# A float64 weight conversion issued as a pipeline over slots, with four load buffers and in-place results, and the attention product moved to the end of a unit

## The chip, the cores and the metric

The kernel runs on one core of a Trainium2 chip. The metric is the time of one execution on the device in microseconds (us). The engines have names of their own: TensorE (PE; its weight loads are listed as PEld), VectorE (DVE), ScalarE (ACT), GpSimd (POOL), and the queue of SyncE (SP), which here only issues DMAs. ScalarE issues some DMAs too (ACTq).

## The reference, cut to what matters

```python
# q, k, v: (8, 8, 576, 64) float32
scores = (q @ k.T) / 8;  keep = scores >= rowmax(scores) - tau          # the rest: -1e9
attn = softmax over the kept;  x = (attn @ v) as (8, 576, 512)
# w_tok1 (576, 256), w_tok2 (256, 576), w_ch1 (512, 1536), w_ch2 (1536, 512): float64
h = relu(x.T @ w_tok1) @ w_tok2;  u = x + h.T
out = u + relu(u @ w_ch1) @ w_ch2
```

The four weight arrays arrive as float64, and the kernel turns them into float32 itself, from their two 32-bit words.

## The kernel before, in words

The program is written out by hand in one order, and every engine executes its own instructions in that order. The main loop (L513) runs over **units**. A unit is a batch, a pair of head pairs, and a tile of 128 query rows; there are 18 units to a batch and 144 in all. Iteration u does, in this order:

- `scores(u)` (L272): the score matmuls (L286) into two PSUM tiles, a maximum for each (L291, VectorE), and from it a bias (L292, GpSimd). The next unit's scores need the same PSUM, so they wait for this unit's L301.
- `norm(u-1)` (L307): two small VectorE steps (L310, L311), and two multiplications on GpSimd (L314).
- The transposed weights of attention for unit u-2. In batch 0 this is `turn`: TensorE transposes (L337) and copies out of PSUM (L339, two or three on VectorE). In later batches it is `turn_blocks`: one VectorE transpose (L348), and, when a group of units is complete, 16 DMAs from the SP queue (L358). GpSimd's `split_middle` (L367) belongs here.
- `fill(0.4)`: from batch 1 on, steps of the mixer of an earlier batch are taken from a queue (`todo`) until a share of the unit's quota is used up. The steps are the transposes of x (`turn_x`, L412, copies on ScalarE L413), `tok1` (L422, L423), `tok2` (L429, its sum on VectorE L433), `ch1` (L451, L452) and `ch2` (L463, L467, L472, store L473). They are priced at 0.44, 4.3, 0.97, 1.7 and 2.6 to 3.0 us.
- `weight(4)`, or `weight(1)` in batch 0: steps of the conversion.
- `weigh(u)` (L295): the two L301 activations and the two exponentials L304 on ScalarE.
- `fill(0.3)`, then the due `values` (L370): the product with v (L388, L393) of a group completed one unit before (batch 0) or two units before, and its copy by ScalarE (L398). After the last one of a batch, `push` puts that batch's mixer steps into `todo` and sets the quota to an even share for 17 units. Then `fill(0.3)`.
- `weight(3)`, or `weight(1)` in batch 0, and then the loads of q, k and v (L106, L114) and the transposes of `prep` (L268).

**The conversion.** There are 31 pieces of at most 128x512 values, each converted in three steps. Each step issues one VectorE instruction, L161, L164 or L167. The first step also issues two ScalarE instructions ahead of it: L159, which scales the low words in the load buffer, and L160, which squares the high words for a test of tiny values. The third step adds the rounding on GpSimd (L168), which writes the weight tile, and then issues the load of the piece three further on (L196, SP queue). That load waits for L168, since it goes into the same buffer. There are three load buffers, two buffers for the result in work, and one for the squares, all in `scratch`. The VectorE steps of a piece wait for its load and for L160; L160 waits for the preceding piece's L167, which reads the one buffer of squares. `need` lets a mixer step force the conversion of its piece.

Of the kernel before, what the change touches and what calls it, by code (L numbers as in the profile page):

```python
# [9 lines left out]
F32 = mybir.dt.float32  # L10
U32 = mybir.dt.uint32
I32 = mybir.dt.int32
I64 = mybir.dt.int64
AF = mybir.ActivationFunctionType
ALU = mybir.AluOpType
# [6 lines left out]
def kernel(  # L22
# [105 lines left out]


# [4 lines left out]
    NRAW = 3  # L134
    raw_at = [scratch[:, 2 * WMAX * i : 2 * WMAX * (i + 1)] for i in range(NRAW)]
    a_at = [scratch[:, 2 * WMAX * NRAW + WMAX * i : 2 * WMAX * NRAW + WMAX * (i + 1)] for i in range(2)]
    sq_at = scratch[:, 2 * WMAX * NRAW + 2 * WMAX : 2 * WMAX * NRAW + 3 * WMAX].bitcast(F32)
    turn_of = [0]

    def like(x, dst):  # L140
        if len(dst.shape) == 2:
            return x
        return x.rearrange("p (a b) -> p a b", a=dst.shape[1])

    def f64_to_f32(dst, raw, rows, n):

        lo, hi = raw[:, :, 0], raw[:, :, 1]
        a = a_at[turn_of[0] % 2][0:rows, 0:n]
        h2 = sq_at[0:rows, 0:n]
        turn_of[0] += 1
        af = a.bitcast(F32)
        nc.scalar.activation(out=lo.bitcast(I32), in_=lo, func=AF.Copy, scale=2.0**-29)  # L159
        nc.scalar.activation(out=h2, in_=hi.bitcast(F32), func=AF.Square)  # L160
        yield nc.vector.tensor_scalar(  # L161
            out=a, in0=hi, scalar1=3, scalar2=0x3FFFFFFF, op0=ALU.logical_shift_left, op1=ALU.bitwise_and
        )
        yield nc.vector.scalar_tensor_tensor(  # L164
            out=a, in0=hi, scalar=0xC0000000, in1=a, op0=ALU.bitwise_and, op1=ALU.bitwise_or
        )
        nc.vector.scalar_tensor_tensor(out=af, in0=h2, scalar=2.0**-30, in1=af, op0=ALU.is_ge, op1=ALU.mult)  # L167
        nc.gpsimd.tensor_tensor(  # L168
            out=dst.bitcast(I32), in0=like(a.bitcast(I32), dst), in1=like(lo.bitcast(I32), dst), op=ALU.add
        )  # L170
# [13 lines left out]

    raws = {}

    def load_piece(i):
        dst, src = pieces[i]
        rows = dst.shape[0]
        n = 1  # L190
        for d in dst.shape[1:]:
            n *= d
        wide = src.dtype == I64
        raw = raw_at[i % NRAW][0:rows, 0 : n * (2 if wide else 1)]
        raw = raw.bitcast(src.dtype)
        nc.sync.dma_start(out=like(raw, dst), in_=src)  # L196
        raws[i] = raw, rows, n

    def weight_ops():
        for i, (dst, src) in enumerate(pieces):  # L200
            raw, rows, n = raws.pop(i)
            if src.dtype == I64:
                for _ in f64_to_f32(dst, raw.bitcast(U32).rearrange("p (n w) -> p n w", w=2), rows, n):
                    yield
            else:
                yield
                yield
                nc.gpsimd.tensor_copy(out=dst, in_=like(raw, dst))
            if i + NRAW < len(pieces):
                load_piece(i + NRAW)  # L210
            yield

    wops = weight_ops()
    steps_done = 0

    def weight(n):

        nonlocal steps_done
        for _ in range(n):
            if next(wops, wops) is wops:  # L220
                return
            steps_done += 1

    def need(i):

        weight(3 * i + 3 - steps_done)
# [6 lines left out]
    load_v(1)  # L233

# [166 lines left out]
    def token_mlp(b):  # L401
# [4 lines left out]
        def turn_x(t):  # L406
            M = MT[t]
            if t == 0:
                s["x"] = work.tile([P, NT, DM], F32, tag="x", bufs=1, name=f"x_{b}")
            ps = ps_tr.tile([P, MAIN], F32, tag="tr", name=f"tx_{b}_{t}").rearrange("p (c x) -> p c x", c=NP)  # L410
            for p in range(NP):
                nc.tensor.transpose(out=ps[0:M, p, :], in_=xT[:, p, o + t * P : o + t * P + M], identity=ident)  # L412
            nc.scalar.copy(out=s["x"][0:M, t, :], in_=ps[0:M].rearrange("q p d -> q (p d)"))  # L413

        def tok1(m):
            need(2)
            if m == 0:
                s["a"] = work.tile([P, NTK, DM], F32, tag="a", bufs=1, name=f"a_{b}")
            ps = ps_mm.tile([P, DM], F32, tag="mm", name=f"t1_{b}_{m}")
            for t in range(NT):  # L420
                M = MT[t]
                nc.tensor.matmul(ps, lhsT=w1[0:M, t, P * m : P * m + P], rhs=s["x"][0:M, t, :], start=(t == 0), stop=(t == NT - 1))  # L422
            nc.scalar.activation(out=s["a"][:, m, :], in_=ps, func=AF.Relu)  # L423
# [89 lines left out]
    for u in range(len(units) + LAG + 4):  # L513
# [11 lines left out]
        if 0 < u <= len(units):  # L525
            norm(u - 1)
        if back:
# [16 lines left out]
        weight(4 if b_now else 1)  # L544
        if on:
            weigh(u)
        if b_now:
            fill(0.3)
        while due and due[0][0] <= u:
            _, b, p, c = due.popleft()  # L550
            values(b, p, c)
            if p == NP - 1 and c == 1:
                push(b)
        if b_now:
            fill(0.3)
        weight(3 if b_now else 1)
# [10 lines left out]
    weight(10000)  # L567
# [30 lines left out]
```

## Time and profile before

| | |
|---|---|
| time, median of 11 runs | 1419.58 us (1418.18 to 1427.12) |
| the profiled execution | 1419.88 us, of which the span is 1417.8 us |
| TensorE busy | 1342.8 us, 95% of the span |
| VectorE, ScalarE, GpSimd busy | 583.7, 588.2 and 345.1 us |
| mean granted TensorE clock | 0.982 |
| L161, L164, L167, mean at 128x512 | 457, 1115 and 712 ns |
| L159, L160, mean at 128x512 | 676 and 665 ns |
| L168, mean at 128x512 | 1350 ns |
| L358: 896 DMAs of 72 KB and 224 of 36 KB | 2.0 and 1.9 us from issue to landing |
| load of a 512 KB weight piece (L196) | 3.7 us from issue to landing |

The page gives each engine's busy time, which says little by itself: most of it lies beside other engines' work. The row of the span in 40 slices (35.4 us each) tells where TensorE isn't busy. The view of waits says who waited for whom, the timeline shows single instructions, and the table by windows gives the busy time of each engine in a stretch. The starts of the score matmuls in the timeline date the units: unit 18, the first of batch 1, starts at 98.56 us, units 19 to 27 at 107.61, 116.08, 130.85, 142.17, 156.95, 171.36, 180.97, 193.79 and 204.88 us.

### The profile page before, as it was taken

The page shows a single profiled execution, that of the slowest core. Times are in us where ns is not written, and L with a number is a line of the kernel's source. Part 1 is how long each engine was busy: PE and PEld are TensorE (multiplying, and loading weights), DVE is VectorE, ACT ScalarE, POOL GpSimd, SP SyncE. Part 2 cuts the span into 40 slices and gives each one's busy share as a digit, 9 for nine tenths or more (in the row PEclk, how much of TensorE's full clock was granted, in tenths as well). Part 3 has the DMA queues.
Part 4 walks back from the last instruction along what each step waited for, and adds up shares of the span by engine and source line. Part 5 has one row for each costly group of instructions (what it writes and reads, how often), then busy time and mean ns, then how long its engine had stood idle before and what let it go on. Part 6 is the DMA issues. An engine that isn't in the chain of part 4 may idle for free.

```text
span 1417.8 us, 19495 instructions
## 1 busy us (share of the span) xinstructions
PE 1342.8 (95%) x6866; PEld 831.0 (59%) x6866; DVE 583.7 (41%) x1009; ACT 588.2 (41%) x1328; POOL 345.1 (24%) x681
## 2 busy tenths in 40 slices
PE   6777699978999999999999999999999999999998
PEld 3444465635656567565656466566656466566675
DVE  5888654344444444434343443434333443201000
ACT  5776453444445444443434454353334344220110
POOL 4565332222222222221221222222122222100000
PEclk8997899999999999999999999999999999999999
DMA  6344544353455434343343434443433433300000
GB/s 135 85 117 127 155 127 104 91 124 80 107 121 115 102 89 105 96 101 85 90 100 81 112 81 114 102 100 72 102 88 79 112 92 78 88 9 15 8 8 23
DMA packets 257376, 128.34 MB, mean 91 GB/s; under 512 B 208064, under 2 KB 221376, under 8 KB 257280
## 3 DMA queue, kind: packets, MB, share of 16 engines
q1 hardware_dynamic: 131632, 111.46, 29.8%
q10 hardware_dynamic: 125648, 15.64, 6.9%
q8 instruction: 55, 0.90, 0.3%
q14 instruction: 41, 0.34, 0.1%
HBM read 43.25 MB, written 9.44 MB: 37 GB/s over the span
## 4 chain that ended last, share of the span: by engine, by line
PE 80%; DVE 7%; SPq 5%; DMA 4%; ACT 3%; issue 1%; POOL 0%; ACTq 0%; DVEq 0%; POOLq 0%
PE c L467 26%; PE c L451 23%; PE sc L286 10%; PE pv L393 7%; SPq L358 5%; PE t L429 3%; PE t L422 3%; PE pv L388 2%; DVE mx L291 2%; DVE T L348 2%; PE tx L412 2%; DMA eT<-T 1%; PE c L463 1%; DMA lk<-in_k_dram 1%; ACT e L301 1%
## 5 line engine op out<-in xcount | busy, mean ns | idle before, releaser
L451 PE MATMUL c<-xT,wc 128*128 128x256 f32 (+1 forms) x1920 | 407.2, 364 | 2.4 <-ACT g L452 1.1
L291 DVE TENSOR_REDUCE mx<-sc 128x1 f32<-128x576 f32 x288 | 204.6, 751 | 486.4 <-PE sc L286 486.3
L467 PE MATMUL c<-wc,g 128*128 128x512 f32 x864 | 389.5, 597 | 0.0
L451 PEld LDWEIGHTS c<-xT,wc 128*128 128x128 f32 x1920 | 332.5, 191 | 76.3 <-issue 29.9
L292 POOL TENSOR_SCALAR bias<-mx,toff 128x1 f32<-128x1 f32 x288 | 76.1, 265 | 804.0 <-DVE mx L291 751.7
L301 ACT ACTIVATE e<-sc,bias 128x576 f32<-128x576 f32 x288 | 198.6, 738 | 169.7 <-POOL bias L292 157.9
L467 PEld LDWEIGHTS c<-wc,g 128*128 128x128 f32 x864 | 157.7, 190 | 177.2 <-issue 175.8
L452 ACT ACTIVATE g<-c 128x256 f32<-128x256 f32 (+1 forms) x240 | 86.8, 362 | 386.9 <-PE c L451 375.7
L304 ACT ACTIVATE e<-e,ntau 128x576 f32<-128x576 f32 x288 | 220.1, 772 | 0.0
L314 POOL TENSOR_SCALAR e<-e,rr 128x576 f32<-128x576 f32 x288 | 213.7, 754 | 17.6 <-DVE rr L311 4.5
L286 PE MATMUL sc<-kT,qT 64*128 64x288 f32 (+1 forms) x1280 | 194.7, 436 | 20.7 <-ACT e L301 11.4
L348 DVE STREAM_TRANSPOSE T<-e 128x1152 f32<-128x1152 f32 x126 | 172.5, 1369 | 16.1 <-DMA eT<-T 12.1
L286 PEld LDWEIGHTS sc<-kT,qT 64*128 64x128 f32 (+1 forms) x1280 | 106.3, 179 | 102.2 <-issue 49.5
L393 PE MATMUL pv<-eT,lv 128*64 128x256 f32 x1024 | 124.3, 386 | 0.0
L472 DVE COPY o<-c 128x512 f32<-128x512 f32 x36 | 24.6, 684 | 192.7 <-PE c L467 192.7
L393 PEld LDWEIGHTS pv<-eT,lv 128*64 128x64 f32 x1024 | 75.8, 140 | 38.6 <-issue 3.2
L429 PE MATMUL t<-w,a 128*128 128x288 f32 x256 | 78.3, 435 | 17.3 <-DVE xT L433 15.4
L422 PE MATMUL t<-x,w 128*128 128x512 f32 (+1 forms) x160 | 75.0, 606 | 0.0
L429 PEld LDWEIGHTS t<-w,a 128*128 128x128 f32 x256 | 46.9, 198 | 42.2 <-DVE xT L433 20.4
L398 ACT COPY xT<-pv 128x256 f32<-128x256 f32 x64 | 23.8, 371 | 108.5 <-PE pv L393 108.4
L433 DVE TENSOR_TENSOR xT<-xT,t 128x288 f32<-128x288 f32 x64 | 27.9, 442 | 95.9 <-PE t L429 95.9
L304 ACT ACTIVATION_READ_ACCUMULATOR e<-e,ntau 128x1 f32 x288 | 56.9, 198 | 0.0
(43 smaller groups left out, 595.9 us busy)
## 6 DMA issues: line engine op xcount, KB each, us to landing
eT<-T SPq DMA_DIRECT2D x896, 72.0 KB, 2.0
scratch<-in_moe_w_ch_dram SPq DMA_DIRECT2D x24, 512.0 KB, 3.7
lv<-in_v_dram SPq DMA_DIRECT2D x32, 288.0 KB, 3.3
out_dram<-o SPq DMA_DIRECT2D x36, 256.0 KB, 2.2
eT<-T SPq DMA_DIRECT2D x224, 36.0 KB, 1.9
lk<-in_k_dram ACTq DMA_DIRECT2D x108, 72.0 KB, 2.7
lq<-in_q_dram ACTq DMA_DIRECT2D x104, 72.0 KB, 2.1
lq<-in_q_dram SPq DMA_DIRECT2D x24, 72.0 KB, 3.3
```

What stands on the lines that cost most here:

```text
L286: nc.tensor.matmul(sc[h][rows, f, 0:HS], lhsT=qT[r, cols], rhs=kT[r, HS * f : HS * f + HS], start=True, stop=True)
L291: nc.vector.tensor_reduce(out=mx[:, c], in_=sc[h][:, :, 0:HS], axis=AX.XY, op=ALU.max)
L301: nc.scalar.activation(out=eh, in_=sc[h][:, :, 0:HS], func=AF.Prelu, bias=bias[:, h : h + 1], scale=SCALE, alpha=STEEP)
L304: nc.scalar.activation(out=eh, in_=eh, func=AF.Exp, bias=ntau, accum_out=rs[:, h : h + 1])
L314: nc.gpsimd.tensor_scalar(out=eh, in0=eh, scalar1=rr[:, h : h + 1], scalar2=1.0, op0=ALU.mult, op1=ALU.mult)
L348: nc.vector.transpose(out=T.rearrange("p (a c n x) -> p c a n x", a=4, c=NK, n=n)[:, :, :, place, :], in_=e.rearrange("p (c a x) -> p c a ...
L393: nc.tensor.matmul(to[r], lhsT=lv[:, j, :], rhs=eT[:, j], start=False, stop=(c == NI - 1), skip_group_check=True)
L422: nc.tensor.matmul(ps, lhsT=w1[0:M, t, P * m : P * m + P], rhs=s["x"][0:M, t, :], start=(t == 0), stop=(t == NT - 1))
L429: nc.tensor.matmul(ps, lhsT=s["a"][:, m, P * c : P * c + P], rhs=w2[:, m, HS * f : HS * f + HS], start=(m == 0), stop=(m == NTK - 1))
L451: nc.tensor.matmul(ps, lhsT=wc1[:, j, c, :], rhs=uT[:, c, GR * i : GR * i + n], start=(c == 0), stop=(c == NCC - 1))
L452: nc.scalar.activation(out=s["g"][:, j, 0:n], in_=ps, func=AF.Relu)
L467: nc.tensor.matmul(flat, lhsT=s["g"][:, j, P * t : P * t + P], rhs=wc2[:, j, :], start=False, stop=(j == NJ - 1), skip_group_check=True)
```

## The change: what it does, and the diff

The conversion becomes a pipeline. A step is a **slot** and issues one VectorE instruction, as before. With it go, in the first slot of piece i, the GpSimd sum of piece i-1 and the load of piece i+3 (there are now four load buffers), and in the second and third slots the two ScalarE instructions of piece i+1. VectorE writes straight into the weight tile, in place. The squares use two buffers, those of the output tile `o`. In batch 0 two slots a unit are issued at the old places. From batch 1 on six are issued, in three pairs: a pair after `norm` and ahead of the transposes, a pair after `fill(0.4)`, and a pair at the end. In this text they are called the first, second and third pair. `values` and `push` stand at the end of the iteration, and one `fill(0.6)` stands for the two of 0.3. `tok1` takes 128 rows for the last tile of tokens too, where it took 64: the other 64 rows of `w1` and of x are zeroed once at the start by GpSimd, and x has a fixed tile.

```diff
+    x_sb = const.tile([P, NT, DM], F32, name="x_sb")
+    nc.gpsimd.memset(x_sb[LAST:P, NI, :], 0.0)
+    nc.gpsimd.memset(w1[LAST:P, NI, :], 0.0)
...
-    NRAW = 3
+    NRAW = 4
...
+        if wide(i):
+            words = raw.bitcast(U32).rearrange("p (n w) -> p n w", w=2)
+            h2 = work.tile([P, WMAX], F32, tag="o", name=f"h2_{i}")[0:rows, 0:n]
+            raws[i] = like(words[:, :, 0], dst), like(words[:, :, 1], dst), like(h2, dst)
...
+    def on_scalar(i, part):
+        if wide(i):
+            lo, hi, h2 = raws[i]
+            if part == 0:
+                nc.scalar.activation(out=lo.bitcast(I32), in_=lo, func=AF.Copy, scale=2.0**-29)
             else:
+                nc.scalar.activation(out=h2, in_=hi.bitcast(F32), func=AF.Square)
...
+                nc.vector.scalar_tensor_tensor(out=dst, in0=h2, scalar=2.0**-30, in1=dst, op0=ALU.is_ge, op1=ALU.mult)
+
+    def on_gpsimd(i):
+        if i >= 0:
+            dst = pieces[i][0]
+            if wide(i):
+                nc.gpsimd.tensor_tensor(out=dst.bitcast(I32), in0=dst.bitcast(I32), in1=raws.pop(i)[0].bitcast(I32), op=ALU.add)
...
     def weight(n):

         nonlocal steps_done
-        for _ in range(n):
-            if next(wops, wops) is wops:
-                return
-            steps_done += 1
+        for k in range(steps_done, min(steps_done + n, 3 * len(pieces) + 1)):
+            i, part = divmod(k, 3)
+            if part == 0:
+                on_gpsimd(i - 1)
+                if i:
+                    load_piece(i - 1 + NRAW)
+            else:
+                on_scalar(i + 1, part - 1)
+            on_vector(i, part)
+            steps_done = k + 1
...
-                M = MT[t]
-                nc.tensor.matmul(ps, lhsT=w1[0:M, t, P * m : P * m + P], rhs=s["x"][0:M, t, :], start=(t == 0), stop=(t == NT - 1))
+                nc.tensor.matmul(ps, lhsT=w1[:, t, P * m : P * m + P], rhs=x_sb[:, t, :], start=(t == 0), stop=(t == NT - 1))
...
         if 0 < u <= len(units):
             norm(u - 1)
+        if b_now:
+            weight(2)
         if back:
...
         if b_now:
             fill(0.4)
-        weight(4 if b_now else 1)
+        weight(2 if b_now else 1)
         if on:
             weigh(u)
         if b_now:
-            fill(0.3)
-        while due and due[0][0] <= u:
-            _, b, p, c = due.popleft()
-            values(b, p, c)
-            if p == NP - 1 and c == 1:
-                push(b)
-        if b_now:
-            fill(0.3)
-        weight(3 if b_now else 1)
+            fill(0.6)
+        weight(2 if b_now else 1)
...
+        while due and due[0][0] <= u:
+            _, b, p, c = due.popleft()
+            values(b, p, c)
+            if p == NP - 1 and c == 1:
+                push(b)
-    weight(10000)
+    need(len(pieces) - 1)
```

## The prediction

> **What bounds the kernel now.** I read the row of slices first, because TensorE (PE) is busy 95% of the span and the question is where the other 75 us lie.
>
> ```profile
> ## 2 busy tenths in 40 slices
> PE   6777699978999999999999999999999999999998
> ...
> PEclk8997899999999999999999999999999999999999
> ```
>
> A slice is 35.4 us. PE misses its nines in the first five slices (to 177 us) and again in slices 10 and 11 (319 to 389 us, the rounded ends of a hole that the timeline puts at 298 to 307 us). From 345 us on it is busy 1063.4 of 1072.8 us: nothing but less PE work helps there. Every microsecond saved ahead of that moves the end by as much. So I cut the early part at the units where the conversion runs.
>
> ```profile
> core 0: us, PE busy (x) PEld busy (x) DVE busy (x) ACT busy (x) POOL busy (x), PEclk, DMA share, GB/s
> 10.00:98.50 88.50, 68.60 (x504) 43.45 (x500) 70.11 (x151) 66.00 (x143) 50.26 (x87) 0.94 0.43 102
> 98.50:204.90 106.40, 81.71 (x390) 52.41 (x388) 77.88 (x121) 59.42 (x123) 48.25 (x63) 0.84 0.50 141
> 204.90:285.00 80.10, 80.10 (x396) 46.84 (x398) 31.55 (x52) 32.33 (x73) 18.77 (x40) 1.00 0.42 100
> ```
>
> Units 18 to 26 (second row) lose 24.7 us of PE, and the clock is at 0.84; as soon as the conversion has ended, PE is full. Who is late there, from the view of waits of that stretch, DVE and PE:
>
> ```profile
> DVE scratch L161 <- DMA scratch<-in_moe_w_ch_dram: 8.8, 3, 4.2
> DVE scratch L167 <- ACT scratch L160: 8.2, 3, 4.4
> ```
> ```profile
> PE t L429 <- DVE xT L433: 10.6, 2, 7.5
> PE sc L286 <- ACT e L301: 6.9, 4, 3.4
> PE tx L412 <- ACT xT L398: 3.7, 1, 3.7
> ```
> ```profile
> SPq L196 <- POOL wc L168: 29.0, 8, 6.6
> ```
>
> VectorE works 77.9 us and stands 17.0 us before its own conversion inputs: it is the engine in front of PE. The reader should see the chain: SP holds a weight load until L168 has freed one of three buffers, behind it 16 issues of L358 take 10 us, the load lands late, L161 stops the VectorE queue, the sums L433 behind it come late, and PE waits 7.5 us at once. One more item, from the timeline (start, length):
>
> ```profile
> 106.31 1.39 POOL L168 TENSOR_TENSOR wc<-scratch 128x512 int32<-128x512 int32 x1 [1.92 <-DVE scratch L167]
> 106.60 1.66 DVE L164 SCALAR_TENSOR_TENSOR scratch<-scratch 128x512 uint32<-128x512 uint32 x1
> ```
>
> L164 takes 0.69 us alone and 1.66 us in ten of its 31 cases, each time beside L168: 0.97 us each.
>
> **What the Trainium skill says.** "SBUF — State Buffer", Who interferes with whom: a VectorE instruction with two SBUF inputs and a GpSimd one that reads SBUF exclude each other for a whole instruction. The two rows above agree. "TensorE: Matmul & The Clock Gate", What's actually happening: after about 3.4 us of idleness the clock falls to half until as much activity has passed. The trace agrees roughly: 0.61 in 116 to 131 us, between waits of 3.38 and 3.65 us. The same page, Architectural detail: VectorE and ScalarE are strictly first in, first out; the late L433 agrees. "DMA: Bandwidth & Descriptors", Anatomy of one DMA: a DMA's semaphore wait is on the issuing sequencer; the SP row above agrees.
>
> **Part by part.** *Prefetch, two buffers of squares, four load buffers.* L159 and L160 now run a piece ahead, and L160 no longer waits for the preceding L167. A load gets seven slots instead of six steps, at six slots a unit instead of seven: 1.17 units instead of 0.86, about 11 us against 8. Behind an L358 group (10 us of issue from about 6 us into a unit, landing 3.7 us) it arrives just in time except once (unit 25, two groups in a row): about 4 us late on ScalarE, 1.5 us of it on PE, as the next scores and one ch1 step lie before it.
>
> *The order of units 18 to 26*, worked out from the new order of each engine with the durations of the trace (scores 1.2, L291 pair 1.42, L310 and L311 0.35, L348 1.36, tok1 4.6, tok2 0.55, ch1 1.85, values 2.4 us). In 18 and 19 VectorE is last: 1.42 + 0.35 + 2 x (0.42 + 0.69 + 0.69) + 1.6 of copies + 1.4 of meetings with GpSimd, some 8 us each: 16.1 together for 17.5 before. Unit 20: no transposes of x stand in it, since `push` comes at its end; 8.4 for 14.8. Unit 21: xT's copy 3.3 after the scores, five transposes paced by ScalarE 3.4, tok1 4.7, and then a new wait of 2.9, because L301 stands behind tok1's Relu and a Square while nothing is left to fill: 14.3 for 11.3. Unit 22: 1.2 + 4.6 + two tok2 with 1.7 of waits for Relu and L301: 8.7 for 14.8. Unit 23: 1.2 + 1.1 to 2.2, then 3.1 of wait, as tok2's PSUM is freed by L433 behind the first pair (1.6 with one meeting) and L348, then four tok2 and values: 12.6 for 14.4. Units 24, 25, 26: 1.2 + 4 x 1.85 = 8.6; 1.2 + 3 x 1.85 + 2.4 = 9.2; 1.2 + 4 x 1.85 + 1.9 = 10.5, for 9.6, 12.8 and 11.1. Sum 88.4; with 1.5 for the late load and 1.5 for a clock that still falls in 18 to 21: 91.4 for 106.4. Gain 15.0; I give it 7 to 22 (half the VectorE stalls gone; or nearly all PE idleness).
>
> *The share of 0.3 that moves.* `push` at the end hands one 1.85 us step to later. It is then done in unit 37, in front of the hole where the product waits 5.05 us for L358's data (16 us after unit 37's scores whatever PE does). So the step costs 1.85 and gets 1.8 back: 0; without the hole +1.85. Within the steady units `values` only changes places with a fill; PE has the same work between L301 and the next scores, so 0. Its DMA slack grows by a third of a fill.
>
> *128 rows in tok1.* In steady stretches a 64-row matmul is followed by the next start after 519 ns in the median (459 in the mean), a 128-row one after 429 (445). Over 32 of them: between 0 (mean) and 2.9 us (median); I take 2.0, as a whole tok1 takes 4.67 against ten of L467's, 4.46. The two memsets lie in GpSimd's first 10.6 us of waiting: 0; exposed, under 0.7 (L121: four in 0.64).
>
> *Batch 0.* PE's and VectorE's orders stay. But six of twelve L168 move behind the two L314 (0.75 each) of the next unit and may meet its L164: up to 6 x 0.97 = 5.8 us worse, of which units with values hide some (VectorE waits 1.7 to 3.5 us for scores in five of them); on the other side, L292 no longer stands behind L168: up to 1 us better. I take 1.5 worse. One load more at the start is 0.4 us of SP beside other loads: 0, or 0.4 exposed.
>
> Sum: 15.0 + 0 + 2.0 - 1.5 = 15.5 less. The profiled execution is 1419.88 us (span 1417.8 and 2.1 around it), 0.3 above the median of the runs: 1404.4.
>
> **The rivals.** *Loads still late* (the L358 issues stay on SP): half the stage's gain, 7.5, with the other terms: 1412. For it: SP's 10 us blocks; against: 11 us of slack. *PE full from unit 20 on*: 22 in the stage, 2.9 of rows, nothing lost in batch 0: 1395. For it: VectorE's own work is under 10 us a unit; against: unit 21's new wait. *It does nothing*, because the chain of reduces, L301 and scores holds the same units: 1419. Against it: 17 us of VectorE stalls have no other cause than buffers. *Slower*: the first pair stands ahead of L348 and L433 in ten units. Its price there is 1.1 us plus a meeting of 0.97 with L314, which starts at that very moment: 2.1 x 10 = 21, plus 5.8 in batch 0, less the 17.0 of stalls and 3.8 for the rest: 1426. It decides if VectorE is last in every unit, that is if its 8 to 9.6 us a unit grow by more than about 1.5; L348 beside L314 (now together) speaks for it, PE's own 8.4 to 12.6 us against.
>
> **How the numbers follow.** Forecast (1399 to 1410) 0.55, loads late (to 1416) 0.16, PE full (1392 to 1399) 0.12, nothing (1417 to 1422) 0.07, slower 0.10. The range from 1394 to 1419 leaves out the slower case and the outer ends of two others, about 0.18. A difference of 0.2% is what a measurement of this kernel can tell from none. Faster 0.83, same 0.07, slower 0.10.
>
> **What would show it.** Units 18 to 26 take about 91 us instead of 106; the two VectorE waits on the load and on L160 fall from 17.0 to under 3; the wait of L429 falls from 10.6 to about 4; a wait of about 3 us for L301 appears ahead of unit 22's scores. The step to 298 us shrinks by 1 to 3 us. Batch 0 up to unit 17 stays within -1 to +6. PE beyond 345 us loses about 2 us. The forecast is wrong if VectorE is busy all through units 20 to 26 or if PE's waits reappear at L348's data.

## The result, and the profile after

The changed kernel takes 1399.67 us (median of 8 runs, 1397.88 to 1402.99) against 1420.33 us (median of 31 runs) of the kernel before: ratio 0.9852, 95% interval 0.9835 to 0.9869, some 21 us less. The forecast was 1404.4 (1394 to 1419). The profiled execution took 1401.33 us; its span is 1399.2 us, 18.6 less than before.

First the page, the row of slices. The slices are now 35.0 us.

```profile
## 2 busy tenths in 40 slices
PE   5776899989999999999999999999999999999998
...
PEclk9998999989999999999999999999999999999999
```

The dip in the first five slices is shallower at its end (the fifth went from 6 to 8), and the gap further on has shrunk from a 7 and an 8 to one 8, the ninth slice (280 to 315 us). Before, it was the ninth and tenth slice; the prediction numbered them one too far, but placed the hole itself rightly by the timeline. Next the table by windows: up to unit 18, units 18 to 26, and the stretch behind (score matmuls of unit 18 start at 101.08 us, of unit 27 at 195.41).

```profile
core 0: us, PE busy (x) PEld busy (x) DVE busy (x) ACT busy (x) POOL busy (x), PEclk, DMA share, GB/s
10.00:101.00 91.00, 70.55 (x504) 44.70 (x504) 70.50 (x151) 66.26 (x143) 50.96 (x87) 0.98 0.45 105
101.00:195.40 94.40, 73.95 (x380) 47.74 (x378) 77.63 (x119) 58.53 (x121) 55.62 (x61) 0.89 0.56 153
195.40:272.00 76.60, 76.60 (x367) 45.76 (x364) 32.84 (x55) 32.17 (x74) 22.53 (x42) 1.00 0.41 98
```

The stage takes 94.4 us instead of 106.4, at the same VectorE work (77.6 and 77.9 us). TensorE still loses 20.5 us in it. Who is late, from the view of waits in that stretch, for VectorE, ScalarE and TensorE:

```profile
DVE wc L209 <- ACT h L193: 2.7, 1, 2.7
DVE wc L201 <- DMA scratch<-in_moe_w_ch_dram: 0.5, 1, 0.5
```
```profile
ACT scratch L191 <- DMA scratch<-in_moe_w_ch_dram: 10.7, 4, 5.8
```
```profile
PE tr L352 <- DVE eT L354: 5.6, 2, 3.0
PE sc L301 <- ACT e L316: 5.2, 2, 3.3
PE tx L425 <- ACT x_sb L426: 3.6, 1, 3.6
PE t L441 <- DVE xT L445: 2.8, 1, 2.8
PE c L463 <- ACT g L464: 2.6, 1, 2.6
```

VectorE waits 3.2 us for its conversion inputs instead of 17.0. The late loads are not gone: they now stop ScalarE, which waits 10.7 us for them, four times. What that does is in the timeline (start, length, and in brackets the idle time before and its releaser), ScalarE and then TensorE, for the load of unit 21 and for that of unit 25 (TensorE has begun unit 26 when it meets the second):

```profile
130.90 0.66 ACT L191 ACTIVATE scratch<-scratch 128x512 int32<-128x512 uint32 x1 [3.56 <-DMA scratch<-in_moe_w_ch_dram]
131.46 1.05 ACT L426 COPY x_sb<-tx 128x512 f32<-128x512 f32 x2
...
187.35 0.69 ACT L191 ACTIVATE scratch<-scratch 128x512 int32<-128x512 uint32 x1 [5.81 <-DMA scratch<-in_moe_w_ch_dram]
```
```profile
132.08 2.86 PE L425 MATMUL tx<-ident,xT 128*128 128x128 f32 x12 [3.57 <-ACT x_sb L426]
134.73 4.56 PE L434 MATMUL t<-x_sb,w 128*128 128x512 f32 x10
141.15 2.34 PE L301 MATMUL sc<-kT,qT 64*64 64x288 f32 x13 [1.86 <-ACT e L316]
...
190.45 3.72 PE L463 MATMUL c<-xT,wc 128*128 128x256 f32 x16 [2.64 <-ACT g L464]
```

The Copy L191 of the next piece stands in ScalarE's queue ahead of the copies of x (L426), and once ahead of a Relu of ch1 (L464). Its load comes 3.56 and 5.81 us late, and TensorE stands for 3.57 and 2.64 us.

The two loads are late for different reasons. First GpSimd and SP's queue at unit 21, then SP's queue at unit 25:

```profile
123.30 1.96 POOL L329 TENSOR_SCALAR e<-e,rr 128x576 f32<-128x576 f32 x2
125.23 3.23 POOL L215 TENSOR_TENSOR wc<-wc,scratch 128x512 int32<-128x512 int32 x2
127.06 0.35 SPq L176 DMA_DIRECT2D scratch<-in_moe_w_ch_dram  x1
```
```profile
173.29 10.01 SPq L373 DMA_DIRECT2D eT<-T  x16
183.42 1.50 SPq L176 DMA_DIRECT2D scratch<-in_moe_w_ch_dram  x3
```

At unit 21 no issue of eT is near. The load goes out when GpSimd's sum (the first of the two L215 merged in that row) has freed its buffer, and the sum stands behind two multiplications of the weights (L329) on GpSimd. At unit 25 the load stands behind sixteen issues of eT.

By the starts of the scores, unit by unit:

| units | 18+19 | 20 | 21 | 22 | 23 | 24 | 25 | 26 | sum |
|---|---|---|---|---|---|---|---|---|---|
| before, us | 17.5 | 14.8 | 11.3 | 14.8 | 14.4 | 9.6 | 12.8 | 11.1 | 106.3 |
| predicted | 16.1 | 8.4 | 14.3 | 8.7 | 12.6 | 8.6 | 9.2 | 10.5 | 88.4, and 3.0 for load and clock |
| after | 15.4 | 6.9 | 17.8 | 10.3 | 14.4 | 8.3 | 8.9 | 12.5 | 94.3 |

The hole at unit 40 shrank as well. These are TensorE's lines before and after:

```profile
307.13 1.12 PE L388 MATMUL pv<-eT,vl 128*64 128x256 f32 x4 [5.05 <-DMA eT<-T]
```
```profile
296.64 1.12 PE L403 MATMUL pv<-eT,vl 128*64 128x256 f32 x4 [1.88 <-DMA eT<-T]
```

### The profile page after: what moved, and what is told of

It is laid out like the page before. It is cut to its first block, busy times and chain, and to the rows that moved or that the text cites. A ratio compares the mean times of both kernels' runs of the same rounds, so it can differ in the third digit from the quotient of the medians.

```text
span 1399.2 us, 19510 instructions
## 1 busy us (share of the span) xinstructions
PE 1329.2 (95%) x6866; PEld 832.7 (60%) x6866; DVE 585.2 (42%) x1009; ACT 588.7 (42%) x1328; POOL 357.8 (26%) x683
## 4 chain that ended last, share of the span: by engine, by line
PE 83%; DVE 7%; SPq 3%; DMA 2%; ACT 2%; issue 1%; POOL 1%; DVEq 0%; ACTq 0%; POOLq 0%
PE c L479 26%; PE c L463 24%; PE sc L301 11%; PE pv L408 7%; PE t L434 4%; PE t L441 3%; SPq L373 3%; DVE mx L306 3%; PE pv L403 3%; DVE T L363 2%; PE tx L425 1%; PE c L475 1%; PE pv_s L408 1%; DMA eT<-T 1%; ACT e L316 1%
## 5 line engine op out<-in xcount | busy, mean ns | idle before, releaser
L306 DVE TENSOR_REDUCE mx<-sc 128x1 f32<-128x576 f32 x288 | 204.8, 752 | 529.2 <-PE sc L301 527.3
L463 PE MATMUL c<-xT,wc 128*128 128x256 f32 (+1 forms) x1920 | 401.7, 362 | 4.7 <-ACT g L464 2.6
L307 POOL TENSOR_SCALAR bias<-mx,toff 128x1 f32<-128x1 f32 x288 | 79.4, 276 | 822.3 <-DVE mx L306 766.7
L316 ACT ACTIVATE e<-sc,bias 128x576 f32<-128x576 f32 x288 | 198.8, 739 | 145.0 <-POOL bias L307 144.7
L464 ACT ACTIVATE g<-c 128x256 f32<-128x256 f32 (+1 forms) x240 | 86.4, 362 | 348.5 <-PE c L463 341.1
L329 POOL TENSOR_SCALAR e<-e,rr 128x576 f32<-128x576 f32 x288 | 218.5, 771 | 16.6 <-DVE rr L326 4.0
L363 DVE STREAM_TRANSPOSE T<-e 128x1152 f32<-128x1152 f32 x126 | 172.5, 1369 | 15.7 <-POOL bias L307 8.7
L441 PE MATMUL t<-w,a 128*128 128x288 f32 x256 | 76.2, 426 | 12.2 <-DVE xT L445 10.1
L434 PE MATMUL t<-x_sb,w 128*128 128x512 f32 x160 | 72.4, 600 | 0.0
L441 PEld LDWEIGHTS t<-w,a 128*128 128x128 f32 x256 | 46.4, 194 | 35.9 <-DVE xT L445 15.2
```

The source lines that it names most:

```text
L306: nc.vector.tensor_reduce(out=mx[:, c], in_=sc[h][:, :, 0:HS], axis=AX.XY, op=ALU.max)
L316: nc.scalar.activation(out=eh, in_=sc[h][:, :, 0:HS], func=AF.Prelu, bias=bias[:, h : h + 1], scale=SCALE, alpha=STEEP)
L329: nc.gpsimd.tensor_scalar(out=eh, in0=eh, scalar1=rr[:, h : h + 1], scalar2=1.0, op0=ALU.mult, op1=ALU.mult)
L363: nc.vector.transpose(out=T.rearrange("p (a c n x) -> p c a n x", a=4, c=NK, n=n)[:, :, :, place, :], in_=e.rearrange("p (c a x) -> p c a ...
L434: nc.tensor.matmul(ps, lhsT=w1[:, t, P * m : P * m + P], rhs=x_sb[:, t, :], start=(t == 0), stop=(t == NT - 1))
L441: nc.tensor.matmul(ps, lhsT=s["a"][:, m, P * c : P * c + P], rhs=w2[:, m, HS * f : HS * f + HS], start=(m == 0), stop=(m == NTK - 1))
```

## The experiments

Two theories stood at the outset. Theory 1, that of the prediction: the gain is the stage of units 18 to 26, because VectorE no longer stops for loads and squares; the moved product gives nothing. Theory 2: the rest, and above all the moved product, carries part of it. The table has every run. Its columns of stages are worked out from the start of each unit's first maximum (L291, L306) in the profiled execution; 45 is a unit of batch 2 that lies behind the hole. The ratio is to runs of the kernel before on the same chip, whose medians were 1419.75 to 1422.96 us. The columns of stages come from single executions on several chips, while the ratio is of medians on one chip; the two differ by up to 6.3 us (e11: 24.7 us by the spans, 31.0 by the medians). The ratio decides on totals, the stages tell the places. How well single executions agree can be seen in the eight runs whose program is the same from unit 45 on (after, e5 to e8 and e10 to e12): 1055.3 to 1056.0 us there, and 144.9 to 147.2 in units 27 to 44.

| run | ratio (95%) | to unit 18 | 18 to 26 | 27 to 44 | from 45 | span |
|---|---|---|---|---|---|---|
| before | 1 | 101.0 | 105.1 | 151.1 | 1060.6 | 1417.8 |
| e1_rows | 0.9964 (0.9950 to 0.9978) | 102.2 | 105.3 | 151.7 | 1058.3 | 1417.5 |
| e2_values_end | 0.9899 (0.9881 to 0.9918) | 101.6 | 101.2 | 147.4 | 1057.7 | 1407.9 |
| e3_conversion | 0.9924 (0.9906 to 0.9942) | 102.9 | 94.2 | 151.8 | 1060.6 | 1409.6 |
| e4_values_mid | 0.9893 (0.9876 to 0.9910) | 102.5 | 91.7 | 151.3 | 1058.4 | 1403.8 |
| **after** | 0.9852 (0.9835 to 0.9869) | 103.6 | 93.1 | 147.2 | 1055.3 | 1399.2 |
| e5_three_buffers | 0.9938 (0.9924 to 0.9951) | 103.9 | 102.5 | 146.3 | 1055.4 | 1408.0 |
| e6_scalar_own_slot | 0.9825 (0.9812 to 0.9839) | 102.7 | 88.3 | 146.5 | 1055.7 | 1393.3 |
| e7_first_pair_late | 0.9920 (0.9907 to 0.9934) | 102.8 | 101.8 | 146.4 | 1055.4 | 1406.4 |
| e8_loads_on_pool | 0.9856 (0.9842 to 0.9869) | 102.3 | 92.9 | 144.9 | 1056.0 | 1396.1 |
| e9_mid_push_end | 0.9897 (0.9878 to 0.9917) | 102.6 | 93.7 | 148.2 | 1059.9 | 1404.5 |
| e10_five_buffers | 0.9804 (0.9786 to 0.9823) | 102.7 | 87.9 | 147.1 | 1055.4 | 1393.1 |
| e11_own_slot_five | 0.9779 (0.9755 to 0.9803) | 104.4 | 86.1 | 146.8 | 1055.7 | 1393.1 |
| e12_pair_late_pool | 0.9846 (0.9824 to 0.9868) | 105.6 | 94.0 | 145.7 | 1056.0 | 1401.3 |

### One part of the change alone

**e1_rows**: the kernel before, with the 128 rows in tok1 and the two memsets.

```diff
-                nc.tensor.matmul(ps, lhsT=w1[0:M, t, P * m : P * m + P], rhs=s["x"][0:M, t, :], start=(t == 0), stop=(t == NT - 1))
+                nc.tensor.matmul(ps, lhsT=w1[:, t, P * m : P * m + P], rhs=x_sb[:, t, :], start=(t == 0), stop=(t == NT - 1))
```

> The kernel before with only tok1's last tile taken over 128 rows. The stretch from unit 45 on got 6.1 us shorter in the changed kernel, and this is the only part that I had priced there. Theory 1 (the price on record, read from starts of neighbouring matmuls): 2.0 us less, ratio 0.9986, with all of it in steps of about 0.18 us per tok1. Theory 2 (the rows carry the whole late gain): about 6 us less, ratio 0.9957. Under theory 1 the other 4 us must come from where the product with v stands.

**e2_values_end**: the kernel before, with the product and `push` at the end of the unit and one fill of 0.6.

```diff
-            fill(0.3)
+            fill(0.6)
-        while due and due[0][0] <= u:
...
-        if b_now:
-            fill(0.3)
         weight(3 if b_now else 1)
...
+        while due and due[0][0] <= u:
...
```

> The kernel before with only the product with v and the push moved to the end of the iteration, and one fill of 0.6; the conversion is the old one. The record gave this move 0. Theory 1 (record): within 2 us, only the hole at unit 38 shrinks by 1.8 and one step moves into it. Theory 2: it saves about 4 us after unit 45 (the product next to the scores, one change of kind of matmul less in each of some 80 units, 50 ns each), 2 us in the hole, and 3 us or more at unit 20, where the transposes of x no longer wait for the copy of xT: 8 to 10 us less, ratio 0.994.

**e3_conversion**: the pipeline over slots with four buffers and its pairs, with 64 rows and the product in the middle.

> The changed kernel with the product with v back in the middle and 64 rows in tok1: only the new conversion is left. Theory 1 (the conversion's buffers and its lead carry the early gain): units 18 to 26 take about 95 us, 9 to 11 us less than 106.3, batch 0 is 2 to 3 us longer, and the whole is 8 to 10 us shorter, ratio 0.994. Theory 2 (the early gain came mostly from the moved push at unit 20): only 2 to 4 us shorter, ratio 0.998. With the two other single parts it shows whether the parts add up to the whole of 0.985.

**e4_values_mid**: the changed kernel with the product and `push` back between the two fills.

> The changed kernel with only the product with v and the push put back between two fills of 0.3. If the move is worth 0 with the new conversion (record), this is within 2 us of the changed kernel, ratio 0.986. If it is worth what its single run shows (4 us after unit 45, 2 in the hole, some at unit 20), it is 6 to 9 us slower than the changed kernel, ratio 0.990 to 0.992.

The rows bring 2.3 us from unit 45 on (1060.6 to 1058.3); e4 against e3 gives 2.2 there. The prediction had 2.0. The ratio of e1 says 5.6 us in the medians, more than its trace has anywhere, and its interval (3 to 7 us) doesn't reach 2.3; what makes up the rest isn't found. The conversion alone brings 10.9 us, all in units 18 to 26 (105.1 to 94.2), and nothing behind. The product and `push` at the end, without the new conversion, bring 3.9 us in that stage, 3.7 in units 27 to 44 and 2.9 from 45 on. So theory 2 of e2 is right in kind, and the ratio, 0.9899, is more than it had. The three don't add up in the stage: both the pipeline and the moved `push` relieve the same units, and with the pipeline the moved part costs 1.4 there (91.7 to 93.1). Theory 1 is right on the stage and wrong on the moved product: it brings 4.1 and 3.1 us behind unit 27 (e4 against after).

### Where the moved product gains

**e9_mid_push_end**: the changed kernel with the product between two fills of 0.3, and only `push` at the end.

```diff
-            fill(0.6)
+            fill(0.3)
+        late_push = []
+        while due and due[0][0] <= u:
+            _, b, p, c = due.popleft()
+            values(b, p, c)
+            if p == NP - 1 and c == 1:
+                late_push.append(b)
+        if b_now:
+            fill(0.3)
...
+        for b in late_push:
+            push(b)
```

> The changed kernel with the product (values) back between the two fills of 0.3, and only push at the end of the unit. It parts the two things that moved together. Theory 1 (the time gained after unit 45 is that of TensorE's turns between kinds of matmul: a product that stands between two fills costs one more turn from the mixer into the scores, 0.09 us each, about 33 of them): units 45 to the end take the same as with both in the middle, 3 us longer than in the changed kernel, and only the hole at unit 40 keeps its gain; total 3 to 4 us slower than the changed kernel (ratio 0.987 to 0.989). Theory 2 (it is push, which hands a share of the work on): like the changed kernel, 0.984 to 0.986, and the time after unit 45 does not grow.

The hole keeps its gain: from unit 39 to 40 it is 8.3 us here, 8.5 in the changed kernel, and 12.3 with `push` in the middle too (e4). So that part belongs to `push`. But `push` alone then gives it all back: against e4 it costs 2.0 us in the stage and 1.5 from unit 45 on, for 3.1 gained in between, and the ratios, 0.9897 and 0.9893, don't differ either. The gain from 45 on belongs to the product: 1059.9 to 1055.3. It isn't in TensorE's waits, which are 6.0 us there in e9 and 7.7 in the changed kernel, so it lies between its matmuls. This is a stretch of the kernel before and one of the changed kernel, in full batches:

```profile
700.97 5.45 PE L451 MATMUL c<-xT,wc 128*128 128x256 f32 x24
706.35 0.65 PE L388 MATMUL pv<-eT,vl 128*64 128x256 f32 x4
706.83 1.90 PE L393 MATMUL pv<-eT,lv 128*64 128x256 f32 x16
708.66 1.99 PE L451 MATMUL c<-xT,wc 128*128 128x256 f32 x8
710.58 1.24 PE L286 MATMUL sc<-kT,qT 64*128 64x288 f32 x8
```
```profile
711.48 2.74 PE L479 MATMUL c<-wc,g 128*128 128x512 f32 x6
714.15 0.65 PE L403 MATMUL pv<-eT,vl 128*64 128x256 f32 x4
714.63 1.90 PE L408 MATMUL pv<-eT,lv 128*64 128x256 f32 x16
716.46 1.24 PE L301 MATMUL sc<-kT,qT 64*128 64x288 f32 x8
```

Before, the product stands between two pieces of ch1, and the scores follow on ch1; after, the scores follow on the product. I took the distance from the start of the last matmul of one kind to that of the first of the next, less the median distance of that shape within its own kind, from unit 45 on: ch1 or ch2 to scores 93 ns more, and into the product 93. The product's matmuls start in pairs, 209 ns from one pair to the next, and what follows the last starts after 309 ns: 100 more.

| from, to | e9: turns x extra = us | after: turns x extra = us |
|---|---|---|
| ch1 or ch2 to scores | 77 x 93 ns = 7.2 | 41 x 93 ns = 3.8 |
| product to scores | 9 x 100 = 0.9 | 44 x 100 = 4.4 |
| product to ch1, ch2, tok1 or tok2 | 36 x 100 = 3.6 | 2 x 100 = 0.2 |
| ch1 or ch2 to product | 38 x 93 = 3.5 | 38 x 93 = 3.5 |

The product costs two turns wherever it stands. At the end it saves the third, from the mixer into the scores: 36 x 0.093 = 3.3 us of the 4.6, and 3.8 with five more turns out of tok1, tok2 and transposes. Another 1.9 lies in distances between matmuls of ch1 and ch2 themselves; why those become shorter isn't shown. What is left of the sum is small, or goes the other way as longer waits.

The weight loads (PEld) of the changed kernel's stretch above show what a turn looks like:

```profile
713.20 0.19 PEld L479 LDWEIGHTS c<-wc,g 128*128 128x128 f32 x1 [0.24 <-issue]
714.15 0.20 PEld L403 LDWEIGHTS pv<-eT,vl 128*64 128x64 f32 x4 [0.76 <-issue]
716.46 0.79 PEld L301 LDWEIGHTS sc<-kT,qT 64*128 64x128 f32 x8 [0.39 <-issue]
```

The load at 713.20 belongs to the matmul that starts 0.43 us later, and runs beside the one ahead of it. The first loads of the product and of the scores start only with their own matmuls, at 714.15 and 716.46. So it is at every turn into or out of scores and product from unit 45 on whose load the trace has, in e9 and in the changed kernel: the load leads its matmul by 3 ns at most. At turns inside the mixer, which cost nothing extra in the median, it leads by 0.2 us in the median. What holds the load back isn't shown. The Trainium skill ("TensorE: Matmul & The Clock Gate", The mechanism) says that a weight load runs beside matmuls in flight only when it goes to other rows of the array. The trace differs: inside the mixer the loads go to all 128 rows, as the matmuls in flight do, and run beside them all the same (713.20 above). Rows alone don't explain the turns either, since the product has 128 rows too.

### How early a load must be issued

**e5_three_buffers** and **e10_five_buffers** change one number, and the fifth buffer is a tile of its own.

```diff
-    NRAW = 4
+    NRAW = 3
```

> The changed kernel with three load buffers in place of four, all else as it is. A load is then issued when the sum of piece i-1 has been queued and is needed by the first ScalarE instruction of piece i+2, four slots (0.67 unit, about 7 us) later; its own time is 3.7 us and the eT issues hold SP for 10 us. Theory 1 (the stage was bound by loads that came late): the late loads multiply, ScalarE's wait for them grows from 10.7 us to over 20 in units 18 to 26, and the kernel is 4 to 8 us slower than with four (ratio to the kernel before about 0.989 to 0.991). Theory 2 (the gain comes from the order of the pairs and from the squares that run ahead; the fourth buffer has little to do with it): within 1.5 us of the changed kernel (0.985 to 0.986).

> The changed kernel with five load buffers (the fifth a tile of its own). Theory 1 (late loads still cost it TensorE's 3.6 us at unit 21 and 2.6 us at unit 25): the waits of ScalarE for loads fall from 10.7 us to under 2 and the kernel is 4 to 6 us faster (ratio about 0.981 to 0.9825). Theory 2 (the next wait behind it, for the exponentials or for xT, takes its place, as when the loads went to GpSimd's queue): less than 2 us (0.984 to 0.986).

**e6_scalar_own_slot** issues both ScalarE instructions of a piece ahead of the piece's own first VectorE instruction; **e11_own_slot_five** does so with five buffers.

```diff
             if part == 0:
                 on_gpsimd(i - 1)
                 if i:
                     load_piece(i - 1 + NRAW)
-            else:
-                on_scalar(i + 1, part - 1)
+                on_scalar(i, 0)
+                on_scalar(i, 1)
             on_vector(i, part)
```

> The changed kernel with the two ScalarE instructions of a piece issued ahead of the piece's own first VectorE instruction, not a piece earlier. Theory 1 (the lead is a part of the gain): VectorE waits about 1.3 us for the square in most of the 28 pieces of units 18 to 26, more where the exponentials or Relus stand ahead on ScalarE; of some 36 us of new waits a fifth reaches TensorE: 4 to 8 us slower in that stage; batch 0 is 1 to 1.5 us faster at its start, since the conversion's instructions no longer stand ahead of unit 1's exponentials. Total +3 to +7 us (ratio 0.987 to 0.990). Theory 2 (VectorE has slack, the lead does nothing after batch 0): -1.5 to +1 us (0.984 to 0.986).

> Five load buffers, and the two ScalarE instructions of a piece ahead of the piece's own first VectorE instruction. If the lead hurts only because a late load then stops ScalarE ahead of the copies of x, the fifth buffer takes the reason away and this is as fast as the changed kernel with five buffers, within 1.5 us. If the lead costs by itself (the two instructions stand ahead of the exponentials and Relus of the pair before), this is 3 us or more faster than that. Against own slot with four buffers (0.9825): 0 to 3 us faster.

A load is issued in the first slot of a piece and first used by L191. Counted in slots, of which a unit has six:

| run | slots from load to use | units 18 to 26, us |
|---|---|---|
| e5, three buffers | 4 | 102.5 |
| after, four buffers | 7 | 93.1 |
| e6, four buffers, own slot | 9 | 88.3 |
| e10, five buffers | 10 | 87.9 |
| e11, five buffers, own slot | 12 | 86.1 |

Four slots, 0.67 unit, cost 9.4 us against seven. Ten save 5.2 us, but not all at the two stops of TensorE. By the starts of the scores, the fifth buffer saves 3.1 us in unit 21, 1.5 in unit 23 and 0.4 in unit 26. The views of waits, ScalarE, with three and with five buffers (where L192 is that Copy and `raw` the fifth buffer), and TensorE with five:

```profile
ACT scratch L191 <- DMA scratch<-in_moe_w_ch_dram: 33.3, 11, 8.8
```
```profile
ACT raw L192 <- DMA raw<-in_moe_w_ch_dram: 4.4, 1, 4.4
```
```profile
184.40 3.72 PE L464 MATMUL c<-xT,wc 128*128 128x256 f32 x16 [2.20 <-ACT g L465]
```

A buffer more sends the load of unit 21 out some 7 us earlier, and that stop is gone. The stop in unit 26 stays, 2.20 us for 2.64: in e10 too a load stands behind sixteen issues of eT, 11.8 us of them from 167.69. So theory 1 of e10 is right on the total, but only one of its two stops went. The 1.5 us of unit 23 are the clock's, as told below under why the prediction held.

The lead of the ScalarE instructions, which I had booked as a help, is a loss with four buffers: it brings the use of a load two slots forward. Without it the stage is 4.8 us shorter and the ratio falls from 0.9852 to 0.9825 (the intervals just meet), the opposite of what theory 1 expected. ScalarE waits as long for loads as in the changed kernel, 10.4 us, but elsewhere. ScalarE and TensorE of e6 at unit 21:

```profile
124.82 0.36 ACT L411 COPY xT<-pv 128x256 f32<-128x256 f32 x1
125.07 0.68 ACT L191 ACTIVATE scratch<-scratch 128x512 int32<-128x512 uint32 x1
125.64 0.68 ACT L193 ACTIVATE h<-scratch 128x512 f32<-128x512 f32 x1
126.27 0.59 ACT L424 COPY x_sb<-tx 128x512 f32<-128x512 f32 x1
```
```profile
125.12 4.00 PE L423 MATMUL tx<-ident,xT 128*128 128x128 f32 x20
128.96 4.46 PE L432 MATMUL t<-x_sb,w 128*128 128x512 f32 x10
```

L191 finds its load there, and the 20 transposes of x run through in 4.00 us instead of stopping for 3.57. With five buffers the lead matters less in the stage: 87.9 against 86.1. The medians of e10 and e11 are 1394.97 and 1391.39 us on one chip, but the intervals of their ratios overlap, so the two aren't told apart. Both beat the changed kernel and the kernel before.

### Which queue holds the loads, and where the first pair stands

**e8_loads_on_pool** issues the loads from GpSimd's queue. **e7_first_pair_late** puts the first pair behind the transposition of the weights. **e12_pair_late_pool** does both.

```diff
-        nc.sync.dma_start(out=like(raw, dst), in_=src)
+        (nc.sync if i < NRAW else nc.gpsimd).dma_start(out=like(raw, dst), in_=src)
```
```diff
-        if b_now:
-            weight(2)
         if back:
...
         if b_now:
+            weight(2)
             fill(0.4)
```

> The changed kernel with the loads of the pieces from the fifth on issued from the GpSimd queue, right behind the sum that frees their buffer, in place of the SP queue, where the issues of eT hold them for 10 us. Theory 1 (the late loads at 130.9 and 187.4 us, which held ScalarE for 3.6 and 5.8 us and TensorE for 3.6 and 2.6, are SP's): ScalarE's wait for loads falls from 10.7 us to under 2 and the kernel is 2 to 5 us faster (0.982 to 0.984). Theory 2 (the issues stand on GpSimd ahead of the biases and the multiplications of the weights, some 0.5 to 1 us each, and what was gained is lost there): within 1 us, or up to 3 us slower.

> The changed kernel with the first pair of slots behind the transposition of the weights and its copies, still ahead of the first fill. The VectorE transpose, and in units 18 and 19 the copies out of PSUM, then come some 1.1 to 2.1 us earlier in each unit. Theory 1 (TensorE and not VectorE is last in units 20 to 26, so the pair costs only the waits for eT in 18 and 19 and for the sum xT at unit 23): 1 to 3 us faster (ratio 0.983 to 0.9845). Theory 2 (the rival of the prediction: the pair ahead is paid in every unit): 8 us or more faster. Slower by 1 to 3 us if the conversion itself is what is late and the pair was well placed.

> The first pair of slots behind the transposition of the weights, as in the run that was 8 to 9 us slower than the changed kernel, but with the loads of the pieces issued from GpSimd's queue, so that the sixteen issues of eT, which then go out ahead of the pair's load, no longer hold it. Theory 1 (that place was slow only because the load of the pair fell behind a group of eT issues on SP): within 2 us of the changed kernel with the loads on GpSimd, ratio 0.984 to 0.987. Theory 2 (the pair is late for VectorE or ScalarE themselves, whatever queue loads it): still 5 us or more slower than that, 0.990 to 0.993.

e7 is 8.7 us slower in the stage than the changed kernel; the rival that the pair ahead of L363 is a cost paid in each unit is refuted with the opposite sign. Here is why, SP's queue and then TensorE in e7 (unit 25):

```profile
172.43 10.01 SPq L373 DMA_DIRECT2D eT<-T  x16
182.54 3.98 SPq L176 DMA_DIRECT2D scratch<-in_moe_w_ch_dram  x4
```
```profile
187.26 3.78 PE L463 MATMUL c<-xT,wc 128*128 128x256 f32 x8 [6.19 <-ACT g L464]
```

The pair's load now stands behind the sixteen issues of eT, which take 10.01 us. Four loads go out in a bunch at 182.54, ScalarE waits 8.04 us for the first, and TensorE 6.19 for ScalarE. With the loads off SP the same place costs little: 94.0 us in e12, 92.9 in e8, and a ratio of 0.9846 against 0.9856. Theory 1 holds for e12. The place ahead of the transposition is worth its 8 to 9 us because it sends the load out ahead of that block: with the loads elsewhere only 1.1 us of it is left.

e8 by itself is no faster than the changed kernel, the outcome of theory 2. ScalarE's waits for loads fall from 10.7 to 6.6 us only, and the two late loads part here. The one of unit 25 no longer stops TensorE: unit 26 takes 9.6 us instead of 12.5. The one of unit 21 still does. ScalarE of e8:

```profile
131.01 0.65 ACT L191 ACTIVATE scratch<-scratch 128x512 int32<-128x512 uint32 x1 [4.24 <-DMA scratch<-in_moe_w_ch_dram]
```

Its load is issued at 126.50, behind the sum as before, and TensorE waits 4.2 us for the copies of x. So the late load of unit 25 is the queue's, and another queue heals it. That of unit 21 is the late sum's, and another buffer heals it.

## Why the prediction held, and where it was off

**The stage of units 18 to 26: right in kind, 12.0 us instead of 15.0.** The waits of VectorE fell from 17.0 to 3.2 us (predicted under 3), and e3 shows 10.9 us from the conversion alone. The wait of tok2 (L441, formerly L429) fell from 10.6 to 2.8 (predicted 4), and the new wait for the exponentials ahead of unit 22 is there at the place named, 1.86 us instead of 2.9, though the Square L193 ahead of L316 held VectorE too (2.7).

**The mis-sized term is "the late load once", 1.5 us.** The load of unit 25 was late as foreseen, by 5.81 us on ScalarE (about 4 predicted) and 2.64 on TensorE (1.5). The load of unit 21, 3.57 us on TensorE, was not foreseen. The count of seven slots was right; what failed was "just in time except once". The forecast set the slots against SP's queue alone and had no term for GpSimd, whose sum must free the buffer first: at unit 21 the load went out at 127.06, and ScalarE, idle from 127.34 on, already wanted it. With five buffers unit 21 takes 14.7 us (scores from 122.26 to 136.99), where 14.3 were predicted. So the order of that unit was worked out right, and most of the 3.5 us that it lacked is this load. I had also taken it for a pure help that "L159 and L160 now run a piece ahead". Experiment e6 shows that with four buffers it cost 4.8 us of the stage, since a strict queue hands a late load on to the copies and Relus behind it. The rival "loads still late" came true in part: the two stops are 6.2 us against the 1.5 booked, 4.7 more, where the rival had 7.5. Its reason, the eT issues on SP, holds for the smaller of the two.

**The clock, 1.5 us**: it still falls, and to less than I thought. Windows of the changed kernel over unit 21, unit 22 and unit 23:

```profile
123.30:141.10 17.80, 11.91 (x38) 6.68 (x38) 14.87 (x19) 8.90 (x18) 12.01 (x13) 0.71 0.42 120
141.10:151.40 10.30, 10.05 (x34) 4.56 (x34) 6.53 (x11) 6.07 (x12) 5.95 (x6) 0.83 0.69 178
151.40:165.80 14.40, 11.63 (x55) 7.73 (x54) 10.76 (x20) 8.02 (x17) 5.42 (x6) 0.88 0.66 177
```

In unit 23 the sixteen matmuls of tok2 behind the wait of 2.77 us take 5.83 us. In e10 the same sixteen, behind a wait of 2.76 us, take 4.33 at a clock of 1.00. So 1.5 of the 1.8 us by which that unit was underestimated are the clock's, and that wait alone doesn't decide whether it falls; units 21 and 22 have more of it.

The prediction read the trace as agreeing roughly with a fall of the clock after 3.4 us of idleness. That reading doesn't stand. In the kernel before the clock is at 0.50 from 108.6 to 112.6 us, ahead of the wait of 3.38 us, and no earlier wait of TensorE in the stage is over 2.2. In the changed kernel it is at 0.50 from 158.9 to 162.2 us, behind the wait of 2.77 us. When it falls isn't settled by these runs.

**One reading was off.** The working takes 0.55 us for a tok2. The trace has two of them, eight matmuls there, in 2.21 us (before, at 158.12), so one takes about 1.0. The terms listed for unit 23 give at most 11.1 us with 0.55, not 12.6; with 1.0 they give 12.9. In unit 22 the error was hidden: of 1.7 us of waits at tok2 0.20 came.

**The share of 0.3 that moves, 0**: for `push` the sum was right (e9 against e4: +2.0, -3.1 and +1.5, together 0.4) and the place of the gain too, the hole. But that the two sides cancel was luck: the cost was booked as one step of 1.85 us at unit 37, and the trace has it in units 18 to 26 and from 45 on. Wrong for the product: "within the steady units `values` only changes places with a fill; PE has the same work, so 0". The matmuls are the same, but not the turns between them. From unit 45 on this brought 3.1 us (e4 against after), or 4.6 (e9 against after); over the whole program the product's move is the difference between e9 and after, 0.9897 to 0.9852, some 6 us of medians. This is the gain that the forecast missed, and it covered the 3 us that it had too much in the stage. The step of the reasoning that failed is the one quoted: that equal work on TensorE takes equal time in any order.

**128 rows, 2.0**: 2.3 from unit 45 on. The reason held too: 64-row matmuls were followed after 519 ns in the median, and those are gone.

**Batch 0, 1.5 worse**: 2.6 worse at unit 18, of which 0.4 lies before unit 0. The size was within the bounds given, but the mechanism was wrong. Most of it (1.8) arises in units 0 to 5, and only one of the first twelve L205 took over 1 us, against two of L164 before, so GpSimd's sum is not the cause. I then thought that the ScalarE instructions of the pipeline stood ahead of unit 1's exponentials; e6 takes this away, and units 0 to 17 take 91.5 us with it and without. Across all runs with the pipeline this stretch lies between 90.9 and 92.9 us (96.1 once, in e12), without it between 89.4 and 90.6. So some 1 to 2 us belong to the pipeline, and their cause stays open.

**The sum.** Predicted from the profiled execution: +1.5 - 15.0 + 0 - 2.0 = -15.5. By the traces: +2.6 in batch 0, -12.0 in the stage, -3.9 in units 27 to 44 (the hole and the turns), -5.3 from 45 on (2.2 rows, 3.1 turns), together -18.6. The total came nearer than its parts: 1.1 and 3.0 us too good in the first two, 7.2 us missed in the last two. That is in part luck.

The rival "PE full from unit 20 on" didn't come true. Two more changes come near it: e11 brings the stage to 86.1, 19 us below before, where the rival had 22, but TensorE still waits 5.3 us for exponentials and 2.6 for tok2's sum. The slower case, which needed VectorE to be last in every unit, has nothing for it: e7 and e12 move the pair behind L363, with no gain.

## What to carry to other kernels

Count how early a load is issued from the instruction that frees its buffer, and against the longest block that can stand ahead of it on its queue, plus its own time. Then ask which engine stops first when it is late: an instruction that is issued a piece ahead on a shared in-order engine moves that stop in front of other work. On a TensorE that is always busy, count the turns between matmuls of different weight shapes, since the order of the same matmuls is worth several us here. Two parts that relieve the same stretch don't add up, so judge each by stages and not by totals alone.

## What the runs showed of the hardware

- A VectorE instruction with one input in SBUF was also held by GpSimd. L201 (one tensor and two constants) takes 0.41 us alone, and 1.51 to 1.52 in five of 31 cases, each time beside L215, which had started 0.56 us or more ahead. I had counted only instructions with two inputs. From the timeline of the changed kernel, VectorE, beside the L215 at 125.23 that the result section shows:

```profile
125.80 1.52 DVE L201 TENSOR_SCALAR wc<-scratch 128x512 uint32<-128x512 uint32 x1
```

  The Trainium skill ("SBUF — State Buffer", Who interferes with whom) has this for instructions in a mode that uses both ports, and counts tensor_scalar, which L201 is, among those that can enter one; whether L201 runs in one isn't to be seen here. L209, with two inputs, showed the same: 1.48 instead of 0.69, twice.
- In e8, where GpSimd issues loads, two of the 31 L205 took 2.16 and 2.17 us, above the 1.66 beside L215 alone, with a DMA issue of GpSimd in progress when they began and an L215 behind it. (A third took 3.52 us, beside two L329 and an L215.) What held the two isn't shown, since other VectorE instructions of e8 ran beside such an issue in their usual 0.69 us: L205 three times and L209 three times.
- A turn of TensorE between the mixer (weights of 128 rows and 128 columns) and the scores (64 rows) or the product (64 columns) costs 93 to 100 ns above the distance within a kind, and the first weight load starts with its matmul instead of ahead of it. A turn inside the mixer, as from ch2 to ch1, costs 0 ns in the median.
